# Input sums one channel pair earlier, the u tile formed on GpSimd, token weights stored permuted

## The chip, the cores and the metric

The kernel runs on one core of one Trainium2 chip. The metric is device time in microseconds for one launch; lower is better. The program works on eight samples one after the other, so most of the time is spent in a steady pattern that repeats once per sample.

## The reference

The input `x` has 8 samples of 3008 tokens and 256 channels, all float32. First a global filter along the tokens, then an MLP mixer: a token product with a residual, then a channel product with a residual.

```python
X = np.fft.rfft(x, axis=1)                     # x: (8, 3008, 256)
Y = X * (filt_r + 1j * filt_i)[None]
x = np.fft.irfft(Y, n=3008, axis=1)
h = np.maximum(x.transpose(0, 2, 1) @ w_tok1, 0.0) @ w_tok2    # w_tok1 (3008, 256), w_tok2 (256, 3008)
u = x + h.transpose(0, 2, 1)
out = u + np.maximum(u @ w_ch1, 0.0) @ w_ch2                   # w_ch1 (256, 1536), w_ch2 (1536, 256)
```

## The kernel before

**The mixer.** `mix` walks over 288 *items* (b, m, jp): sample b (0 to 7), block m of 512 tokens (0 to 5, the last of 448), and pair jp of 128-wide tiles of the hidden channels (0 to 5). The products are 2 by 2 block products done with seven multiplications instead of eight, so sums and differences of operands and of results have to be made by VectorE (the helper `v`, L997). In one item TensorE does, in this order: `up_first` (L1019, four products into two banks called pg), part 0 of `down` for the item before, `up_last` (L1035, three products into the same two banks), part 1 of `down` and part 2 of `down` (L1053). VectorE in the same item does `up_middle` (tiles hh and s, read from pg), the sums t of the item before (`h_sums`: one of 512 elements, two of 256, all from the on-chip tile hh), and two results hh out of pg. ScalarE copies one result and takes the two ReLUs.

Between these stand places (0, 1, 1.5, 1.7, 2) at which `mix` yields, and at which other work is put in:

- The next block's operand u, made at jp = 2 and 3 by `u_quarter` in parts 0 to 3 (at jp = 4 for the first block of the next sample). Its even and odd parts come out of PSUM by VectorE; `u_turn` (L943 to L953) then turns them in place into their sum and difference with two VectorE instructions of 512 elements; `v_steps` makes the sums v out of u. `u_turn` and `v_steps` are put into a list, and `one_step` takes two entries of it per item, after `up_last`.
- The finished block's results (`finish`): four steps of sums and two transposes, then 16 stores whose DMAs are issued by GpSimd (L1065) at jp = 2 and 3.
- The filter of the sample after next, `dft`, from sample 1 on beside the mixer. Its first stage has six channel pairs of input. For each, `next_sum` has VectorE make sum and difference of two loaded tiles (L563, two instructions of 512 elements; the results, tiles p1 and p2, alternate), then loads another pair on SyncE's queue; `sets` multiplies them (L538 on sd, eight products of quarter arrays) into two banks, either the pg pair or the pair acc and b (`turn`); ScalarE copies the banks out, SyncE stores them to z. Later stages (steps "b", "m", "i") have two sets per channel quad.

Which filter step comes at which place is written by hand in the last lines of the kernel: a table gives (jp, place) for each step, and `tail` is the last block of a sample. The letters are those that `dft` yields: "s" a sum, "e" a single pair's sets, "d" two pairs' sets, "c" the copies out of acc and b, "w" loads of filters and tables.

Before the change the first stage runs so: sum 0 at (3, 1) and sets 0 at (4, 1.5) of the tail; sums 1 and 2 at (0, 1) and (1, 1), sets 1 and 2 together at (1, 1.5) of the next sample's first block; sums 3 and 4 at (2, 1) and (3, 1), sets 3 at (3, 1.5) on the pg banks; sum 5 at (4, 1) and sets 4 and 5 at (4, 1.5).

**The token product** (`token_product`) runs once per sample at jp = 2 of the last block, from weights in `w1_d`, a scratch tensor in DRAM. `w1_sums` writes it during sample 0: the raw rows and the sums that GpSimd makes of them, in eight DMAs issued by GpSimd. `w1_load` reads it back, twelve slices per sample, each in two DMAs on SyncE's queue, one for each half of the partitions, with the rows permuted on the way.

Of the kernel before, what the change touches and what calls it, by code (L numbers as in the profile page):

```python
# [10 lines left out]
FP32 = mybir.dt.float32  # L11
# [3 lines left out]
ALU = mybir.AluOpType  # L15


B = 8
# [5 lines left out]
P = 128  # L24
# [19 lines left out]
JP = JT // 2  # L44
DH = D // P
CW = 32
CB = P // CW
MT = 6
# [5 lines left out]
W1S = 7  # L54
# [78 lines left out]
def kernel(  # L133
# [11 lines left out]
    nc = tc.nc  # L145
# [19 lines left out]
    w1_d = nc.dram_tensor("w1_tmp", (AP, P, 7, P), FP32, kind="Internal").ap()  # L165
# [14 lines left out]
    up = pool("up", 2)  # L180
    hp = pool("hp", 2)
    tp = pool("tp", 2)
    vp = pool("vp", 2)
# [10 lines left out]
    turn = ["acc", "b"]  # L194
# [17 lines left out]
    w1_ring = w1_all.rearrange("p (r s t) -> p r s t", s=7, t=P)  # L212
# [327 lines left out]
    def half_of(half, n=HALF):  # L540
        return slice(half * HALF, half * HALF + n)
# [34 lines left out]
    def dft(bs):  # L576
        first = bs[0] == 0
# [21 lines left out]
        def zero_rows(c):  # L599
            nc.gpsimd.memset(filts[c], 0.0)  # L600

        def w_load(c):
            table_load(c)
            (filt_load if first else filt_quad)(c)
# [15 lines left out]
        def next_sum():  # L620
            i = len(sums)
            sums.append(x_sums(*todo[i], i))
            more(1)

        def sets(i, n, banks_of):
            return [a_pair(*u, sd, tags) for u, sd, tags in zip(todo[i:i + n], sums[i:], banks_of)]

        if tiled:
            next_sum()
            for i in (0, 3):  # L630
                yield "e"
                sets(i, 1, (("pg", "pg"),))[0]()
                for _ in range(2 if i == 0 else 1):
                    yield "s"
                    next_sum()
                yield "d"
                leave, leave_pg = sets(i + 1, 2, (turn, ("pg", "pg")))
                leave_pg()
                yield "c"
                leave()  # L640
                for _ in range(2 * (i == 0)):
                    yield "s"
                    next_sum()
                    if len(sums) == 4:
                        zero_rows(0)
                        w_load(0)
            yield "w"
        for i, u in enumerate(() if tiled else todo):
            if first and i in (0, 2):
# [152 lines left out]
    def w1_sums():  # L802

        w = w1.rearrange("p (j r) (t n) -> p j r t n", r=2, n=P)
        to = w1_d.rearrange("j p s n -> p j s n")

        def raw_out():
            nc.gpsimd.dma_start(to[:, :, 0], w[:, :, 0, 0])
            nc.gpsimd.dma_start(to[:, :, 1:3], w[:, :, 1])

        def pool(out, in0, in1, op):
            return lambda: nc.gpsimd.tensor_tensor(out=out, in0=in0, in1=in1, op=op)

        todo = [raw_out]
        for j in range(0, AP, 3):
            c11, c21, c12, c22 = (w[:, j:j + 3, r, t] for r in range(2) for t in range(2))
            todo += [pool(c22, c21, c22, ALU.add), pool(c21, c11, c21, ALU.subtract),
                     pool(c11, c22, c11, ALU.subtract), pool(c12, c12, c11, ALU.subtract)]

        def sums_out(j):  # L820
            return lambda: nc.gpsimd.dma_start(to[:, j:j + 2, 3:7], w[:, j:j + 2].rearrange("p j r t n -> p j (r t) n"))

        return todo, [sums_out(j) for j in range(0, AP, 2)]

    def w1_load(j):
        rows = w1_d[j].rearrange("(k h g) s n -> h k g (s n)", h=2, g=2)
        for h in range(2):
            nc.sync.dma_start(w1_ring[half_of(h), j % W1S], rows[h])

    token_ts, todo_h1 = {}, []  # L830

# [47 lines left out]
    def width(m):  # L879
        return 512 if m < MT - 1 else 448  # L880
# [8 lines left out]
    def u_unit(b, m, h1, ut, dh):  # L889

        w = width(m)
        ps = bank(free_bank())
        for t in range(TC):
            nc.tensor.matmul(ps[:, 0:w], h1[:, t, ts(dh, P)], w2[:, t, ds(m * 512, w)],
                             start=(t == 0), stop=False)
        u_filter(b, m, dh, ps, False)
        nc.scalar.copy(out=ut[:, dh, 0:w], in_=ps[:, 0:w])
# [42 lines left out]
            for e in range(2):  # L940
                v(us[:, :, e], pss[e], us[:, :, e])

    def u_turn(ut):  # L943
        us = ut.rearrange("p d (e n) -> p d e n", e=2)
        plus, minus = us[:, :, 0], us[:, :, 1]

        def first():
            v(plus, plus, minus)

        def second():  # L950
            nc.vector.scalar_tensor_tensor(out=minus, in0=minus, scalar=-2.0, in1=plus, op0=ALU.mult, op1=ALU.add)

        return [first, second]  # L953

    def w2m_load(m):
        nc.sync.dma_start(w2m[m % 2], w2_d[m])
# [39 lines left out]
    def v(out, in0, in1, op=ALU.add):  # L996
        nc.vector.tensor_tensor(out=out, in0=in0, in1=in1, op=op)  # L997
# [7 lines left out]
    def u_sums(ut, vt, w):  # L1005
        hw = w // 2
        return sums(vt[:, :, 0:hw], ut[:, :, hw:w], ut[:, 0, 0:w].rearrange("p (s n) -> p s n", s=2),
                    ut[:, 0, 0:hw], ut[:, 1, 0:hw])
# [138 lines left out]

    def u_part(b, m, i):
        if i == 0:
            uts[b, m] = up.tile([P, DH, 512], FP32, tag="u", name="u")  # L1150
        (u_quarter if b else u_unit)(b, m, h1s[b], uts[b, m], i)

    def v_steps(b, m):
        vts[b, m] = vp.tile([P, 4, 256], FP32, tag="v", name="v")
        t13, t2, t4_ = u_sums(uts[b, m], vts[b, m], width(m))

        def t24():
            t2()
            t4_()

        return [t13, t24]

    todo_v = []

    def one_step():
        if todo_v:
            todo_v.pop(0)()

    def mix(next_ready):
# [14 lines left out]
        def u_parts(b, m, jp, place):  # L1184
            parts = own[b > 0] if m + 1 < MT else new if b + 1 < B else {}
            now = parts.get((jp, place), ())
            b, m = (b, m + 1) if m + 1 < MT else (b + 1, 0)
            for part in now:
                u_part(b, m, part)
            if now and now[-1] == max(p for ps in parts.values() for p in ps):  # L1190
                if m:
                    wait.append(m)
                if b:
                    todo_v.extend(u_turn(uts[b, m]))
                todo_v.extend(v_steps(b, m))
                if b and (b, m) < (B - 1, MT - 2):
                    w2m_load((m + 2) % MT)
# [5 lines left out]
        for i in range(len(items) + 1):  # L1203
# [70 lines left out]
            if now:  # L1274
                if b + 1 < B and i % n == n - 4:
                    h1s[b + 1] = yield from token_product(b + 1)
                u_parts(b, m, jp, 2)
                if m + 1 == MT and jp == JP - 2 and b + 1 < B:
                    one_step()
                    one_step()  # L1280
                if jp == JP - 1:
                    while todo_v and m + 1 == MT:
                        one_step()
                if i >= 8 and to_dram:
                    to_dram.pop(0)()
                if i in (28, 29):
                    w2m_load(i - 28)
                if i == 28:
                    nc.sync.dma_start(wai[:, 0:HALF], was_i_d)
# [5 lines left out]
    with tc.manual_schedule():  # L1295
# [71 lines left out]
        for b, i, place in mix(next_ready):  # L1367
            at = (b, i, place)
            if at == (0, 0, 0) or group + 1 < len(GROUPS) and at == (GROUPS[group][-1], n - 4, 2):
                if not done:  # L1370
                    raise AssertionError("the filter's steps don't fit beside the mixer's")
                group += 1
                done = group + 1 == len(GROUPS)
                todo = iter(()) if done else dft(GROUPS[group + 1]) if group else second
                coming = next(todo, "end") if group else "a"
                if group:
                    continue
            if done or place == 1.7 and coming != "m":
                continue
            jp = i % JP  # L1380
            if coming in "aw":
                due = place == 1 or (place != 1.5 if group == 0 else coming == "w")
            else:
                tail = i >= n - JP
                due = i >= JP * (group == 0) and (jp, place) in {
                    "s": ((3, 1),) if tail else ((0, 1), (1, 1), (2, 1), (3, 1), (4, 1)),
                    "e": ((4, 1.5),) if tail else ((3, 1.5),), "d": ((1, 1.5), (4, 1.5)), "c": ((2, 0), (5, 0)),
                    "b": ((1, 1.5), (4, 1.5)), "m": ((2, 1.7) if tail else (3, 1), (5, 1)), "i": ((0, 1.5), (4, 1.5))}[coming]
            if coming == "a" and group == 0 and i < JP - 1:
                due = place in (0, 2)  # L1390
            for _ in range(due):
                if not done:
                    coming = next(todo, "end")
                    done = coming == "end"
# [30 lines left out]
```

## Time and profile before

| | |
|---|---|
| Runs | 2453.93, 2454.04, 2458.0 us; median 2454.04 us |
| Profiled execution | 2460.43 us, of which the span of the trace is 2458.7 us |
| Granted TensorE clock over the span | 0.993 |
| Busy share of the span | TensorE 97%, VectorE 82%, GpSimd 29%, ScalarE 28% |
| VectorE, `u_turn`'s two instructions | 42 x 682 ns and 42 x 692 ns |
| GpSimd, issue of an output store | 738 x 623 ns |
| GpSimd, sum of 512 elements per partition (L966) | 18 x 1350 ns |

The page gives the busy time of each engine, the time cut into slices, DMA queues and the costliest groups of instructions. A group's line ends with the idle time of its engine just before its instructions and what ended that idle time. The view of waits lists the same by waiter and releaser: us in total, how often, the longest. A timeline lists instructions in order of time: start, duration and, in square brackets, the idle time before it with its releaser; a float32 matmul leaves two records, so "x8" are four products. TensorE's durations overlap, because matmuls are pipelined: two records of 128x256 that follow one another start 0.216 us apart at full clock, and 0.427 us apart at half clock.

### The profile page before, as it was taken

To read this page: it belongs to the slowest core of one execution; us is meant where nothing else is said; L and a number is where in the kernel's file an instruction comes from. 1 tells how busy PE (TensorE), PEld (TensorE's weight loads), DVE (VectorE), ACT (ScalarE), POOL (GpSimd) and SP (SyncE) were. 2 spreads that over 40 slices of the span, in tenths; PEclk is the share of its full clock that TensorE was granted. 3 is DMA by queue.
4 is the path that set the end of the run, shared out by engine and by line. 5 is a ranking of instruction groups with operands and counts; after the bars stand their busy time and mean duration, and the time that the engine had idled before them with its cause. 6 is when DMAs were issued, how large, how long until landed. Compare 5 with 4: busy or idle time off the path is not lost.

```text
span 2458.7 us, 41273 instructions
## 1 busy us (share of the span) xinstructions
PE 2379.9 (97%) x15148; PEld 1983.3 (81%) x15148; DVE 2011.5 (82%) x3753; ACT 689.4 (28%) x1339; POOL 705.6 (29%) x1117
## 2 busy tenths in 40 slices
PE   7989999999999999999999999999999999999998
PEld 4667678778897888978888788877888788898887
DVE  7798887778877888778887788877887788878786
ACT  5732222222222222222221222222222222212222
POOL 7486644121221122212212221222122112212222
PEclk8999999999999999999999999999999999999999
DMA  9964347343463334533345433644346333441101
GB/s 213 247 179 138 119 140 211 111 126 89 108 188 121 99 102 128 172 117 96 108 125 152 128 106 98 177 116 124 92 108 187 116 105 101 129 130 30 48 14 21
DMA packets 191088, 302.35 MB, mean 123 GB/s; under 512 B 44100, under 2 KB 127402, under 8 KB 185510
## 3 DMA queue, kind: packets, MB, share of 16 engines
q1 hardware_dynamic: 144238, 237.62, 33.2%
q0 software_dynamic: 40032, 55.28, 9.5%
q10 hardware_dynamic: 6616, 6.82, 0.9%
q8 instruction: 120, 1.97, 0.4%
q14 instruction: 82, 0.67, 0.1%
HBM read 215.40 MB, written 83.62 MB: 122 GB/s over the span
## 4 chain that ended last, share of the span: by engine, by line
PE 71%; DVE 10%; DMA 9%; POOL 4%; issue 3%; ACT 2%; SPq 1%; DVEq 0%; ACTq 0%; POOLq 0%
PE ps_po L1053 28%; PE ps_pg L1019 16%; PE ps_pg L1035 12%; PE ps_acc L925 3%; DVE t L997 3%; PE ps_pg L538 3%; PE ps_b L538 2%; POOL out_dram L1065 2%; DMA z_tmp<-t 2%; DVE hh L997 2%; PE ps_b L925 2%; DMA out_dram<-r 1%; DVE u L997 1%; PE ps_b L851 1%; PE ps_acc L905 1%
## 5 line engine op out<-in xcount | busy, mean ns | idle before, releaser
L1065 POOL DMA_DIRECT2D out_dram<-r x738 | 453.3, 623 | 1536.6 <-issue 981.2
L1040 ACT ACTIVATE hh<-hh 128x512 f32<-128x512 f32 (+1 forms) x576 | 347.7, 621 | 1017.8 <-DVE hh L997 1014.0
L997 DVE TENSOR_TENSOR hh<-ps_pg,s 128x512 f32<-128x512 f32 (+3 forms) x864 | 481.6, 585 | 153.6 <-ACT s L1022 143.8
L1053 PE MATMUL ps_po<-t,wc 128*128 128x256 f32 (+1 forms) x2296 | 566.8, 381 | 3.4 <-DVE t L997 3.3
L1053 PEld LDWEIGHTS ps_po<-t,wc 128*128 128x128 f32 x2296 | 426.6, 191 | 97.2 <-issue 32.2
L1019 PE MATMUL ps_pg<-v,wc 128*128 128x256 f32 (+1 forms) x1728 | 418.8, 379 | 7.0 <-DVE v L997 5.3
L1053 PE MATMUL ps_po<-hh,wc 128*128 128x256 f32 (+1 forms) x1722 | 411.9, 375 | 0.6 <-POOL wc L396 0.6
L1019 PEld LDWEIGHTS ps_pg<-v,wc 128*128 128x128 f32 x1728 | 326.1, 191 | 57.1 <-DVE v L997 19.1
L1053 PEld LDWEIGHTS ps_po<-hh,wc 128*128 128x128 f32 x1722 | 327.4, 190 | 38.3 <-POOL wc L396 1.4
L1035 PE MATMUL ps_pg<-u,wc 128*128 128x256 f32 (+1 forms) x1152 | 292.6, 377 | 7.4 <-DVE hh L997 7.3
L997 DVE TENSOR_TENSOR t<-t,hh 128x256 f32<-128x256 f32 (+1 forms) x576 | 254.9, 442 | 19.8
L1035 PEld LDWEIGHTS ps_pg<-u,wc 128*128 128x128 f32 x1152 | 216.1, 190 | 41.8 <-DVE hh L997 15.3
L997 DVE TENSOR_TENSOR s<-ps_pg,hh 128x512 f32<-128x512 f32 (+1 forms) x288 | 196.0, 681 | 30.7 <-DVE hh L997 0.9
L1022 ACT COPY s<-ps_pg 128x256 f32<-128x256 f32 (+1 forms) x288 | 105.9, 368 | 337.9 <-PE ps_pg L1019 336.1
L997 DVE TENSOR_TENSOR t<-hh 128x512 f32<-128x512 f32 (+1 forms) x288 | 196.4, 682 | 0.6 <-ACT hh L1040 0.6
L1019 PE MATMUL ps_pg<-u,wc 128*128 128x256 f32 (+1 forms) x576 | 171.2, 379 | 6.6 <-DVE hh L997 3.9
L1035 PE MATMUL ps_pg<-v,wc 128*128 128x256 f32 (+1 forms) x576 | 168.8, 375 | 0.0
L1019 PEld LDWEIGHTS ps_pg<-u,wc 128*128 128x128 f32 x576 | 108.2, 191 | 26.3 <-DVE hh L997 8.4
L997 DVE TENSOR_TENSOR u<-ps_acc,u 128x256 f32<-128x256 f32 x84 | 46.8, 557 | 98.6 <-PE ps_acc L925 76.1
L1035 PEld LDWEIGHTS ps_pg<-v,wc 128*128 128x128 f32 x576 | 108.4, 190 | 13.4
L925 PE MATMUL ps_acc<-w 128*128 128x256 f32 x336 | 97.5, 392 | 0.0
L717 DVE TENSOR_TENSOR p<-ps_b,filt 128x1024 f32<-128x1024 f32 x56 | 68.4, 1222 | 14.5 <-PE ps_pg L538 11.4
(169 smaller groups left out, 2801.6 us busy)
## 6 DMA issues: line engine op xcount, KB each, us to landing
w<-w_tmp SPq DMA_DIRECT2D x42, 1024.0 KB
w<-w_tmp SPq DMA_DIRECT2D x168, 224.0 KB
out_dram<-r POOLq DMA_DIRECT2D x738, 32.0 KB, 4.3
g_tmp<-t SPq DMA_DIRECT2D x112, 192.0 KB
t<-g_tmp SPq DMA_DIRECT2D x42, 512.0 KB
t<-z_tmp SPq DMA_DIRECT2D x196, 96.0 KB
z_tmp<-t SPq DMA_DIRECT2D x72, 256.0 KB
wb<-wbi_t SPq DMA_DIRECT2D x56, 256.0 KB
```

What stands on the lines that cost most here:

```text
L538: nc.tensor.matmul(outs(i, j), stat(i, j), mov(i, j), start=True, stop=True)
L717: nc.vector.tensor_tensor(out=prods[c, h], in0=pss[h].unsqueeze(1).to_broadcast([P, 2, 2, D]), in1=filts[c % FB], op=ALU.mult)
L851: nc.tensor.matmul(ps[:, at], w[:, n], mov, start=(j == 0 and i in (0, 2)), stop=(j == AP - 1 and i >= 5))
L905: nc.tensor.matmul(pss[e][half_of(i), dh, ts(q, HALF)], t4[b, c][half_of(e), r, ds(dh * P + i * HALF, HALF)], wai[half_of(e), 0:HALF], sta ...
L925: nc.tensor.matmul(to, h1[:, n, :], w2_at(m, at), start=(i < 2 and j == 0), stop=(j >= 1))
L997: nc.vector.tensor_tensor(out=out, in0=in0, in1=in1, op=op)
L1019: nc.tensor.matmul(ps[:, 0:hw], chan[0][:, jp, n, :], mov, start=True, stop=True)
L1022: nc.scalar.copy(out=s[:, 0], in_=g[0][:, 0, 0:hw])
L1035: nc.tensor.matmul(ps[:, 0:hw], chan[0][:, jp, n, :], mov, start=True, stop=True)
L1040: nc.scalar.activation(out=hs, in_=hs, func=AF.Relu)
L1053: nc.tensor.matmul(po[i][:, j, 0:hw], chan[1][:, jp, n, :], mov, start=(jp == 0 and first == 1), stop=(jp == JP - 1 and last == 1))
L1065: q.dma_start(bass.AP(tensor=ob.tensor, offset=ob.offset + to, ap=ap + [[1, cw]]), of)
```

## The change

1. In `dft`, sums 0 and 1 stand before the first sets, and from then on every sum stands one pair further ahead. The table's "s" becomes (3, 1), (4, 1), (5, 1) in the tail and (0, 1), (2, 1), (3, 1) otherwise, its "e" becomes (4, 1.5) and (5, 1.5), without regard to the tail. Sets 1 then run alone in the tail, on acc and b; sets 2 and 3 together at (1, 1.5), sets 4 and 5 together at (4, 1.5). Clearing and loading the first filter tile (`zero_rows(0)`, `w_load(0)`) moves from after sum 3 to after sets 3.
2. From sample 1 on, `u_quarter` writes the even and odd parts into the tile that will hold v, and GpSimd makes u from them with two instructions (sum and difference, 512 elements each), issued right after the parts. `v_steps` then overwrites the even and odd parts. The two VectorE steps, and the two `one_step` calls that made room for them at the sample's end, go.
3. `w1_sums` writes the rows of `w1_d` in the order in which they are read, four DMAs for each one before (32 in all), on SyncE's queue; `w1_load` is one DMA.

```diff
         if tiled:
             next_sum()
-            for i in (0, 3):
+            yield "s"
+            next_sum()
+            for i in range(2):
                 yield "e"
-                sets(i, 1, (("pg", "pg"),))[0]()
-                for _ in range(2 if i == 0 else 1):
+                sets(i, 1, (turn if i else ("pg", "pg"),))[0]()
+                yield "s"
+                next_sum()
+            for i in (2, 4):
+                yield "d"
+                leave, leave_pg = sets(i, 2, (turn, ("pg", "pg")))
+                leave_pg()
+                if i == 2:
+                    zero_rows(0)
+                    w_load(0)
+                yield "c"
+                leave()
+                for _ in range(2 * (i == 2)):
                     yield "s"
                     next_sum()
-                yield "d"
...
-                    if len(sums) == 4:
-                        zero_rows(0)
-                        w_load(0)
             yield "w"
...
         def raw_out():
-            nc.gpsimd.dma_start(to[:, :, 0], w[:, :, 0, 0])
-            nc.gpsimd.dma_start(to[:, :, 1:3], w[:, :, 1])
+            for i in range(4):
+                nc.sync.dma_start(to[i][:, :, 0], w[i::4, :, 0, 0])
+                nc.sync.dma_start(to[i][:, :, 1:3], w[i::4, :, 1])
...
     def w1_load(j):
-        rows = w1_d[j].rearrange("(k h g) s n -> h k g (s n)", h=2, g=2)
-        for h in range(2):
-            nc.sync.dma_start(w1_ring[half_of(h), j % W1S], rows[h])
+        nc.sync.dma_start(w1_ring[:, j % W1S], w1_d[j])
...
-    def u_turn(ut):
-        us = ut.rearrange("p d (e n) -> p d e n", e=2)
-        plus, minus = us[:, :, 0], us[:, :, 1]
-
-        def first():
-            v(plus, plus, minus)
-
-        def second():
-            nc.vector.scalar_tensor_tensor(out=minus, in0=minus, scalar=-2.0, in1=plus, op0=ALU.mult, op1=ALU.add)
-
-        return [first, second]
+    def u_turn(b, m):
+        plus, minus = (vts[b, m].rearrange("p d (e n) -> p d e n", e=2)[:, :, e] for e in range(2))
+        uts[b, m] = up.tile([P, DH, 512], FP32, tag="u", name="u")
+        us = uts[b, m].rearrange("p d (h n) -> p d h n", h=2)
+        return [lambda: nc.gpsimd.tensor_tensor(out=us[:, :, 0], in0=plus, in1=minus, op=ALU.add),
+                lambda: nc.gpsimd.tensor_tensor(out=us[:, :, 1], in0=plus, in1=minus, op=ALU.subtract)]
...
                 if b:
-                    todo_v.extend(u_turn(uts[b, m]))
+                    for f in u_turn(b, m):
+                        f()
                 todo_v.extend(v_steps(b, m))
...
-                if m + 1 == MT and jp == JP - 2 and b + 1 < B:
-                    one_step()
-                    one_step()
...
-                    "s": ((3, 1),) if tail else ((0, 1), (1, 1), (2, 1), (3, 1), (4, 1)),
-                    "e": ((4, 1.5),) if tail else ((3, 1.5),), "d": ((1, 1.5), (4, 1.5)), "c": ((2, 0), (5, 0)),
+                    "s": ((3, 1), (4, 1), (5, 1)) if tail else ((0, 1), (2, 1), (3, 1)),
+                    "e": ((4, 1.5), (5, 1.5)), "d": ((1, 1.5), (4, 1.5)), "c": ((2, 0), (5, 0)),
```

More of the change, by code (lines that the diff above doesn't have):

```diff
@@ L629, in dft @@
             next_sum()
-            for i in (0, 3):
+            yield "s"
+            next_sum()
+            for i in range(2):
                 yield "e"
-                sets(i, 1, (("pg", "pg"),))[0]()
-                for _ in range(2 if i == 0 else 1):
+                sets(i, 1, (turn if i else ("pg", "pg"),))[0]()
[11 more added lines that the diff above has]
+                for _ in range(2 * (i == 2)):
                     yield "s"
                     next_sum()
-                yield "d"
[L637 to L643, printed above, removed]
-                    if len(sums) == 4:
-                        zero_rows(0)
-                        w_load(0)
             yield "w"
@@ L804, in w1_sums @@
         w = w1.rearrange("p (j r) (t n) -> p j r t n", r=2, n=P)
-        to = w1_d.rearrange("j p s n -> p j s n")
+        to = [w1_d.rearrange("j (h k g) s n -> h g k j s n", h=2, g=2)[i // 2, i % 2] for i in range(4)]
         def raw_out():
-            nc.gpsimd.dma_start(to[:, :, 0], w[:, :, 0, 0])
-            nc.gpsimd.dma_start(to[:, :, 1:3], w[:, :, 1])
+            for i in range(4):
+                nc.sync.dma_start(to[i][:, :, 0], w[i::4, :, 0, 0])
+                nc.sync.dma_start(to[i][:, :, 1:3], w[i::4, :, 1])
         def pool(out, in0, in1, op):
@@ L820, in sums_out, with f @@
         def sums_out(j):
-            return lambda: nc.gpsimd.dma_start(to[:, j:j + 2, 3:7], w[:, j:j + 2].rearrange("p j r t n -> p j (r t) n"))
+            def f():
+                for i in range(4):
+                    nc.sync.dma_start(to[i][:, j:j + 2, 3:7], w[i::4, j:j + 2].rearrange("p j r t n -> p j (r t) n"))
+            return f
         return todo, [sums_out(j) for j in range(0, AP, 2)]
     def w1_load(j):
-        rows = w1_d[j].rearrange("(k h g) s n -> h k g (s n)", h=2, g=2)
-        for h in range(2):
-            nc.sync.dma_start(w1_ring[half_of(h), j % W1S], rows[h])
+        nc.sync.dma_start(w1_ring[:, j % W1S], w1_d[j])
     token_ts, todo_h1 = {}, []
@@ L1149, in u_part @@
         if i == 0:
-            uts[b, m] = up.tile([P, DH, 512], FP32, tag="u", name="u")
-        (u_quarter if b else u_unit)(b, m, h1s[b], uts[b, m], i)
-    def v_steps(b, m):
-        vts[b, m] = vp.tile([P, 4, 256], FP32, tag="v", name="v")
-        t13, t2, t4_ = u_sums(uts[b, m], vts[b, m], width(m))
+            where, tag = (vp, "v") if b else (up, "u")
+            to = uts if b == 0 else vts
+            to[b, m] = where.tile([P, DH, 512], FP32, tag=tag, name=tag)
+        if b:
+            u_quarter(b, m, h1s[b], vts[b, m], i)
+        else:
+            u_unit(b, m, h1s[b], uts[b, m], i)
+    def v_steps(b, m):
+        if b == 0:
+            vts[b, m] = vp.tile([P, 4, 256], FP32, tag="v", name="v")
+        vt = vts[b, m] if b == 0 else vts[b, m].rearrange("p d (s n) -> p (d s) n", s=2)
+        vts[b, m] = vt
+        t13, t2, t4_ = u_sums(uts[b, m], vt, width(m))
         def t24():
```

## Prediction, made before the changed kernel was run

> **What bounds the kernel now.** I read the page first, then the waits of TensorE, then timelines of single stretches, and last the start times of every item's first up product (L1019 on u).
>
> ```profile
> PE 2379.9 (97%) x15148; PEld 1983.3 (81%) x15148; DVE 2011.5 (82%) x3753; ACT 689.4 (28%) x1339; POOL 705.6 (29%) x1117
> ```
>
> TensorE is the bound, so only its waits can be won. The view of waits says whom it waits for:
>
> ```profile
> PE ps_pg L538 <- DVE sd L563: 17.4, 12, 1.7
> ...
> PE ps_pg L1035 <- DVE hh L997: 7.3, 10, 1.6
> PE ps_pg L1019 <- DVE v L997: 5.3, 7, 0.8
> ...
> PE ps_pg L1019 <- ACT t L554: 2.8, 6, 1.1
> PE ps_b L851 <- DMA w<-w_tmp: 2.4, 4, 0.9
> ```
>
> The largest is the input sets waiting for their sums, twice in each of six samples. The timelines of TensorE and VectorE show such a place, jp = 1 of a first block:
>
> ```profile
> 1053.48 0.65 PE L538 MATMUL ps_b<-sd,was 64*64 64x512 f32 x2
> ...
> 1056.30 1.59 PE L538 MATMUL ps_pg<-sd,was 64*64 64x512 f32 x8 [1.73 <-DVE sd L563]
> 1057.82 1.96 PE L1053 MATMUL ps_po<-t,wc 128*128 128x256 f32 x4
> 1059.58 1.06 PE L1019 MATMUL ps_pg<-u,wc 128*128 128x256 f32 x2
> ```
> ```profile
> 1053.14 1.28 DVE L997 TENSOR_TENSOR hh<-ps_pg,s 128x512 f32<-128x512 f32 x2
> 1054.34 1.22 DVE L997 TENSOR_TENSOR u<-u,r 128x224 f32<-128x224 f32 x3
> 1055.47 1.28 DVE L563 TENSOR_TENSOR sd<-filt 128x512 f32<-128x512 f32 x2
> ```
>
> The banks pg are free when the hh results are out, at 1054.42; the sets start 1.88 us later, behind sum 2. After the wait TensorE also runs at half clock (two products in 1.96 us instead of 1.03), for 3.41 us. That happens in three of six samples.
>
> The item lengths, from one first up product to the next, are very regular. A plain item takes 6.04 us (sample 7, where no filter runs); one with filter sets "b" 8.13. Against that, jp = 0 of a block takes 6.24: TensorE waits 0.20 for v, hidden in pipelined records. jp = 0 of a sample's first block takes 6.70. jp = 1 of the first block takes 11.02 (11.82, 12.51 and 12.67 with half clock), and jp = 4 there 10.35 to 11.30, mean 10.65.
>
> **The change, part by part.** The sum is made against the profiled execution, 2460.43 us (span 2458.7, 1.7 around it). The median of the runs is 6.4 lower. The half-clock stretches make 5.0 of that if the median run lacks them: 1.64, 0.79 and 1.48 over 11.03, and 0.90 and 0.16 more in the items behind the last two.
>
> *Sums ahead.* Sum 2 moves to (5, 1) of the tail, sum 3 to (0, 1), sum 5 to (3, 1). Only the pg banks then hold the second set back. At jp = 1 the gap from the end of the acc and b sets (last start 1053.98, plus 0.47) to 1056.30 is 1.85 us; 0.6 more lies in small waits of that item, of which I take half: 2.15 x 6 samples = 12.9 us. At jp = 4 the same gap is 1.29; the mean of 10.65 holds 0.25 more of waits on ScalarE's copies, and small ones: 1.7 x 6 = 10.2. Without any wait both items would be 6.04 + 0.96 (acc and b) + 1.40 (pg) + 0.15 = 8.55 us, so the ends are 14.8 and 12.6, and 0 if pg comes late anyway. Sets 1 leave jp = 3 (10.77 against 9.49, so 1.28 us) for the tail, where a set on acc and b is about 1.05, with its two z stores (SyncE, 0.7 us each): 0.
>
> *Half clock.* It follows the longest of these gaps, and goes with them: 5.0 in the profiled execution, 0 against the median. [...]
>
> *What the moved sums push.* Two sums (1.28 us each) now stand in the tail at jp = 4 and 5, one at jp = 0. At jp = 4 VectorE idles 3.59 us right there, which hides the first; without that cover it would hold up the parts of u behind it by 1.28. The other two have `finish` behind them, whose results nothing waits for, and then `up_middle`, which TensorE does wait for. Adding up VectorE's instructions from 1041 us on, it reaches jp = 1 some 0.6 us late for `up_last`: 0.6 x 6 = 3.6 us, between 0 and 7. Each sum issues its six loads earlier on SyncE's queue (0.60, 0.51, 0.26 us, twice); behind them are w2 and z transfers, and TensorE's waits above name none of those: 0. The first filter tile is cleared (0.97 us) ahead of the 16 stores on GpSimd, no longer behind them, and SyncE's loads of it, which waited up to 12.2 us for that, come earlier: 0.
>
> *u on GpSimd.* VectorE loses 42 x (682 + 692) ns = 57.7 us, worth something only where TensorE waits for it. v moves from the end of jp = 5 to the end of jp = 4, an item before it is needed: 0.20 x 35 blocks = 7.0 us. At a sample's start v stays at jp = 5, with less in front of it: half of 0.66 x 7, 2.3 us.
>
> The price is what GpSimd's sums do to VectorE's. Sample 0 has the row, on GpSimd and on VectorE:
>
> ```profile
> 383.74 4.14 POOL L966 TENSOR_TENSOR w<-w 128x512 f32<-128x512 f32 x3
> ```
> ```profile
> 383.55 2.03 DVE L997 TENSOR_TENSOR t<-hh 128x512 f32<-128x512 f32 x1
> 385.61 2.56 DVE L997 TENSOR_TENSOR t<-t,hh 128x256 f32<-128x256 f32 x2
> 388.09 1.27 DVE L997 TENSOR_TENSOR hh<-ps_pg,s 128x512 f32<-128x512 f32 x2
> ```
>
> The t sums, whose operands are both on chip, take 4.6 us instead of 1.57; hh, with an operand in PSUM, is untouched. Each GpSimd sum on top of t costs VectorE about 1.0 us. Where would the new ones lie? In block 2 of sample 2, at the end of jp = 3, the last part of the next u is out at 878.26, and GpSimd is still issuing stores:
>
> ```profile
> 868.78 4.37 POOL L1065 DMA_DIRECT2D out_dram<-r  x8 [34.42 <-ACT u L931]
> 873.81 5.46 POOL L1065 DMA_DIRECT2D out_dram<-r  x8 [0.66 <-DMA out_dram<-r]
> ```
>
> It is free at 879.27; over the blocks, 0.1 to 2.4 us after u's last part, mostly 0.5 to 1.2. Two sums of 1.35 us end at about 882. The t sums of jp = 4 run from 880.29 to 881.9, so the second GpSimd sum lies on them, the first hardly: VectorE is late by 1.0 us, between 0 (done before t) and 2.7 (both fully in front of t). hh is out at 883.09, and the sets that follow on pg start at 883.82, so 0.73 are covered. 30 items have such sets (four blocks with "b" and one with input sets, six samples): 30 x (1.0 - 0.73) = 8.1 us. In sample 7's five there is 1.35 us of cover: 0. VectorE asks for u at 883.1 + 1.0, GpSimd is done at 882: no wait there.
>
> [...] In the row VectorE's instructions end 0.3 to 0.6 us after GpSimd's, so they overlap in part. [...]
>
> *Token weights.* 84 loads on SyncE instead of 168; TensorE waits 2.4 us for them in all: 0, at most 2.4 won. The 32 writes (0.4 us each, 12.8 us of queue) replace eight issues on GpSimd (6.5 us). The first eight stand before loads of z for which SyncE waits until 198.7 us anyway, the others in stretches where it idles (304.8 to 316.5): 0, up to 3 if that cover fails.
>
> Sum: 12.9 + 10.2 + 7.0 + 2.3 - 3.6 - 8.1 = 20.7 us off the median, 2454.0 - 20.7 = 2433.3; with the half clock 25.7 off the profiled execution, 2434.7. I say 2434.
>
> **Rivals.** *GpSimd's sums lie on t.* If the stores keep GpSimd longer, or its sums run slower than 1.35 us, VectorE is late by 2.7 in each jp = 4: 30 x 1.97 + 5 x 1.35 = 66 us against the other terms' 28.8, so 37 slower, 2491. It decides from a delay of 0.73 + 28.8 / 30 = 1.69 us on. For it speaks the row above, where three sums cost 3.0; against it that hh and s read PSUM, and that the first sum falls on those. 9%.
>
> *The wait only changes its name.* [...] For it speaks VectorE at 82%; against it the 1.88 us between hh's end and the set's start. 10%.
>
> *Sums don't move ahead.* The order of instructions excludes it: sum 3 stands a whole item before sets 2 and 3 on VectorE. 1%.
>
> **How the numbers follow.** The forecast has 80%. Its low end, with all waits gone and no lock, is 2454.0 - (14.8 + 12.6 + 7.0 + 4.6) = 2415; I take 2418. The upper end reaches to the rivals' first part, 2456, and leaves out the case of 2491. A measurement can tell about 0.2%, 4.9 us, from no change: faster 0.80, same 0.10, slower 0.10.
>
> **What would show it.** L538's wait for sd gone from TensorE's waits, and jp = 1 and 4 of first blocks at 8.6 to 9.2 us; jp = 0 at 6.04; no half clock inside the mixer; GpSimd's two sums ending before VectorE's v; the t sums of jp = 4 longer by about 1 us, and "b" items there at 8.4. Wrong would be "b" items at jp = 4 above 9 us, or L538 waiting for hh instead of sd for over 10 us.

## The result

The changed kernel takes 2414.49 us, the median of 4 runs (2412.96 to 2415.46), against 2455.15 (2453.93 to 2458.0) for the kernel before: a ratio of 0.9832, 95% interval 0.9815 to 0.9849. The medians are 40.7 us apart where 20.7 were forecast; the profiled executions (2460.43 and 2413.99 us) are 46.4 apart, forecast 25.7. The direction was right, the range did not hold the time: 2414 lies below its low end of 2418.

**The profile after.** The page's line of engines: VectorE has lost 84 instructions but only 12 us of busy time, because others of its instructions became longer, its t sums above all (the first of the three in each item: 196.4 us before, 233.0 now, over all items).

```profile
PE 2361.0 (98%) x15148; PEld 1979.2 (82%) x15148; DVE 1999.9 (83%) x3669; ACT 689.9 (29%) x1339; POOL 805.5 (33%) x1193
```

TensorE's waits. "L538 <- DVE sd" (17.4 us before) is gone, and little stands in its place: the sets now wait for hh, 2.6 us in all. The wait for v fell from 5.3 to 0.8.

```profile
PE ps_po L1053 <- DVE t L997: 5.7, 13, 0.7
...
PE ps_pg L1035 <- DVE hh L997: 5.0, 6, 1.4
...
PE ps_pg L538 <- DVE hh L997: 2.6, 6, 1.0
...
PE ps_pg L1019 <- DVE v L997: 0.8, 1, 0.8
```

The timeline of TensorE at jp = 1 of the same first block as before (sample 3). The set on pg now starts 0.43 us after the one on b and acc instead of behind a gap, and the next part of `down` follows 1.09 us later, at full clock:

```profile
1036.09 0.59 PE L538 MATMUL ps_b<-sd,was 64*64 64x512 f32 x2
...
1036.52 1.16 PE L538 MATMUL ps_pg<-sd,was 64*64 64x512 f32 x8
1037.61 1.13 PE L1053 MATMUL ps_po<-t,wc 128*128 128x256 f32 x4
1038.58 0.59 PE L1019 MATMUL ps_pg<-u,wc 128*128 128x256 f32 x2
```

Item lengths (first up product to next first up product), after minus before, summed over samples 1 to 6 of the two profiled executions, beside the forecast's terms sorted into the same places:

| Items | Forecast, us | Measured, us |
|---|---|---|
| jp = 1, 2 of first blocks (half clock included) | -17.9, pushed sums +3.6 | -17.9 |
| jp = 4 of first blocks | -10.2, GpSimd's sums +1.6 | -15.2 |
| start of a sample: jp = 5 of the tail, jp = 0 and 3 of the first block | -2.3 | -7.1 |
| jp = 0 of later blocks (v earlier) | -7.0 | -5.7, and -0.95 in sample 7 |
| jp = 1 of later blocks | 0 | -2.5 |
| jp = 4 of blocks 1 to 4 (GpSimd's sums) | +6.5 | +16.5 |
| jp = 2, 3 of the tail | 0 | -6.5 |
| sample 0, and what stands before it | 0 | -6.3 |
| sum | -25.7 | -45.7 of the 46.4 |

jp = 1 is now 8.82 to 9.12 us, jp = 4 of the first block 8.12, jp = 0 of a sample 5.67. No stretch at half clock is left in samples 1 to 6.

### The profile page after: what moved, and what is told of

It is laid out like the page before. It is cut to its first block, busy times and chain, and to the rows that moved or that the text cites. A ratio compares the mean times of both kernels' runs of the same rounds, so it can differ in the third digit from the quotient of the medians.

```text
span 2412.2 us, 41264 instructions
## 1 busy us (share of the span) xinstructions
PE 2361.0 (98%) x15148; PEld 1979.2 (82%) x15148; DVE 1999.9 (83%) x3669; ACT 689.9 (29%) x1339; POOL 805.5 (33%) x1193
## 3 DMA queue, kind: packets, MB, share of 16 engines
q1 hardware_dynamic: 148014, 243.12, 32.6%
q10 hardware_dynamic: 6616, 6.82, 0.9%
## 4 chain that ended last, share of the span: by engine, by line
PE 83%; DVE 9%; DMA 3%; issue 2%; POOL 1%; ACT 1%; SPq 0%; DVEq 0%; ACTq 0%; POOLq 0%
PE ps_po L1053 32%; PE ps_pg L1019 18%; PE ps_pg L1035 13%; PE ps_acc L930 3%; PE ps_b L856 3%; DVE t L997 3%; PE ps_pg L538 3%; PE ps_b L538 3%; PE ps_acc L856 2%; PE ps_b L930 2%; DVE hh L997 2%; PE ps_acc L910 1%; DVE s L997 1%; DVE sd L563 1%; DMA x<-in_x_dram 1%
## 5 line engine op out<-in xcount | busy, mean ns | idle before, releaser
L1019 PE MATMUL ps_pg<-v,wc 128*128 128x256 f32 (+1 forms) x1728 | 412.6, 375 | 2.2 <-POOL wc L395 1.5
L997 DVE TENSOR_TENSOR t<-t,hh 128x256 f32<-128x256 f32 (+1 forms) x576 | 259.9, 451 | 19.8
L997 DVE TENSOR_TENSOR t<-hh 128x512 f32<-128x512 f32 (+1 forms) x288 | 233.0, 809 | 0.6 <-ACT hh L1040 0.6
L1035 PE MATMUL ps_pg<-v,wc 128*128 128x256 f32 (+1 forms) x576 | 168.8, 375 | 0.0
L997 DVE TENSOR_TENSOR v<-ps_acc,v 128x256 f32<-128x256 f32 x84 | 46.9, 558 | 85.2 <-PE ps_acc L930 61.4
L997 DVE TENSOR_TENSOR u<-ps_po,u 128x512 f32<-128x512 f32 (+1 forms) x142 | 79.1, 585 | 0.0
```

Source lines behind the costliest of these rows:

```text
L1019: nc.tensor.matmul(ps[:, 0:hw], chan[0][:, jp, n, :], mov, start=True, stop=True)
L1035: nc.tensor.matmul(ps[:, 0:hw], chan[0][:, jp, n, :], mov, start=True, stop=True)
```

## The experiments

**The three parts, alone and in pairs.** Six kernels divide the change: part 1 is the input sums, part 2 u on GpSimd, part 3 the token weights. Each is the kernel before with those hunks of the change. Each ratio here and further down is to runs of the kernel before that were taken together with that experiment's (medians 2456.05, 2456.95 and 2457.01 us), so the ratios, not the medians, are to be compared across tables.

Part 1 alone:

```diff
-            for i in (0, 3):
+            yield "s"
+            next_sum()
+            for i in range(2):
...
-                    "s": ((3, 1),) if tail else ((0, 1), (1, 1), (2, 1), (3, 1), (4, 1)),
+                    "s": ((3, 1), (4, 1), (5, 1)) if tail else ((0, 1), (2, 1), (3, 1)),
```

> Only the first part of the change: sums one pair ahead, u still turned by VectorE, w1 as before. Theory A (the sets waited for their sums, and each part removes its own waits): jp = 1 of first blocks falls from 11.0 to 12.7 us to about 8.9, jp = 4 from 10.65 to 8.2 to 8.6, no half clock in the mixer, jp = 0 stays at 6.24; 25 to 32 us off, 2423 to 2430. Rival B (VectorE as a whole was late, and its relief by GpSimd is what did it): the sets then wait for hh on the pg banks, jp = 4 stays above 9.5, no more than 12 us off, 2443 or more.

Part 2 alone:

```diff
-                    todo_v.extend(u_turn(uts[b, m]))
+                    for f in u_turn(b, m):
+                        f()
...
-                    one_step()
-                    one_step()
```

> Only the second part: GpSimd forms u, sums and w1 as before. [...] Rival B (VectorE's 58 us less work is what shortens the waits elsewhere): 10 us or more faster, 2445 or less.

Part 3 alone:

```diff
-        for h in range(2):
-            nc.sync.dma_start(w1_ring[half_of(h), j % W1S], rows[h])
+        nc.sync.dma_start(w1_ring[:, j % W1S], w1_d[j])
```

> Only the third part: w1 written permuted on SyncE, read with one DMA. Theory A (the 6.5 us that the changed kernel lost at jp = 2 and 3 of the tails, and part of sample 0's 4, come from the loads): those items at 24.15 and 5.30, 6 to 10 us off, 2445 to 2449. Rival B (these tails are shorter because VectorE and GpSimd are ahead): no change, 2455 within 2.

Parts 1 and 2 (the changed kernel with the third diff undone):

```diff
-        nc.sync.dma_start(w1_ring[:, j % W1S], w1_d[j])
+        for h in range(2):
+            nc.sync.dma_start(w1_ring[half_of(h), j % W1S], rows[h])
```

> First and second part without the third. Theory A (the third part is worth the tail's 6.5 us and some of sample 0): 2421 to 2424. Rival B (it is worth nothing): 2414 to 2416.

Parts 1 and 3 (the changed kernel with the second undone):

```diff
-                    for f in u_turn(b, m):
-                        f()
+                    todo_v.extend(u_turn(uts[b, m]))
```

> First and third part without the second: VectorE turns u as before. [...] Rival B (without the relief VectorE is late for the pg banks in first blocks and at the samples' start): 2420 or more.

Parts 2 and 3 (the changed kernel with the first undone):

```diff
-                    "s": ((3, 1), (4, 1), (5, 1)) if tail else ((0, 1), (2, 1), (3, 1)),
+                    "s": ((3, 1),) if tail else ((0, 1), (1, 1), (2, 1), (3, 1), (4, 1)),
```

> Second and third part without the first. If the parts add, this is the changed kernel plus what the first part is worth alone: with 25 to 32 us for that, 2440 to 2447. If the sums ahead work only together with GpSimd's u, 2425 to 2435.

| Parts | Median, us | Ratio to before, 95% interval |
|---|---|---|
| 1 | 2417.89 | 0.9837 (0.9819 to 0.9856) |
| 2 | 2471.23 | 1.0053 (1.0036 to 1.0070) |
| 3 | 2445.20 | 0.9947 (0.9931 to 0.9963) |
| 1, 2 | 2425.14 | 0.9869 (0.9851 to 0.9888) |
| 1, 3 | 2408.53 | 0.9803 (0.9787 to 0.9820) |
| 2, 3 | 2461.04 | 1.0016 (1.0007 to 1.0025) |
| 1, 2, 3 | 2414.49 | 0.9832 (0.9815 to 0.9849) |

What follows:

- Part 1 makes nearly the whole gain. Its items alone change by -18.3 (jp = 1, 2), -15.2 (jp = 4) and -7.8 us (start of a sample): the first three rows of the table, without any relief by GpSimd.
- Part 2 costs 0.3 to 0.7% in all four comparisons (against nothing, part 1, part 3, and both); the two of 0.3% are little more than their intervals. Its items show both sides: -5.7 at jp = 0, -2.5 at jp = 1, and +16.3 at jp = 4 of blocks 1 to 4. Without part 1 it is worst: alone it makes jp = 4 of the first block 5.7 us longer in six samples. Most of that is half clock: four of these six items have a stretch with a granted clock of 0.5 for 3.41 us and take 11.65 to 12.34 us, the other two 10.70 and 11.16. In the kernel before no such stretch falls there.
- Part 3 brings 0.3 to 0.5% wherever it is added: 4.0 to 6.4 us at jp = 2 and 3 of the tails of samples 1 to 6, and 4.2 to 6.7 us in sample 0, of which 1.1 to 2.7 in its tail.
- The expectation held for part 3 (2445 to 2449), and parts 1 and 3, at 2408.53, contradict the rival's 2420 or more. Part 1 was faster than its 2423 to 2430, parts 1 and 2 were a little slower than their 2421 to 2424, and part 2 alone, at 2471.23, is far from its rival's 2445 or less. Parts 2 and 3 missed by most: 14 us above the 2440 to 2447, because part 1 is worth more beside them (1.8%) than the 25 to 32 us put in for it.

How part 1 shortened the start of a sample can be read in two timelines of TensorE. Before, the first item of sample 3 stood 0.76 us before its v products:

```profile
1041.06 0.60 PE L1019 MATMUL ps_pg<-u,wc 128*128 128x256 f32 x2
1042.41 1.56 PE L1019 MATMUL ps_pg<-v,wc 128*128 128x256 f32 x6 [0.76 <-DVE v L997]
```

After, sets 1 stand in the item ahead, and the v products follow at once:

```profile
1022.39 0.59 PE L538 MATMUL ps_b<-sd,was 64*64 64x512 f32 x2
...
1022.93 1.02 PE L1053 MATMUL ps_po<-t,wc 128*128 128x224 f32 x4
1023.79 0.59 PE L1019 MATMUL ps_pg<-u,wc 128*128 128x256 f32 x2
1024.22 1.46 PE L1019 MATMUL ps_pg<-v,wc 128*128 128x256 f32 x6
```

jp = 0 is 5.67 us with part 1 alone too, where VectorE still turns u. So the moved set did not add its length: it gives TensorE work while VectorE makes v, where TensorE stood idle. In six samples jp = 3 lost 7.7 us and jp = 0 6.2, and jp = 5 of the tail gained 6.75.

**Who holds up VectorE.** In the changed kernel GpSimd issues the output stores of the finished block first and u's sums after them. This kernel issues the stores of blocks 0 to 3 behind the sums:

```diff
+            if b and m < MT - 2:
+                held.append(send)
+            else:
+                send()
...
                     for f in u_turn(b, m):
                         f()
+                    while held:
+                        held.pop(0)()
```

> The changed kernel, but for blocks 0 to 3 the 16 stores are issued after GpSimd's two sums instead of before. Theory A (the stores hold GpSimd until 0.5 to 2.4 us after u's parts, and so its sums meet VectorE's t sums): GpSimd's sums start 0.15 us after the parts in every block, VectorE's first t sum ends at about +3.2 instead of up to +4.2, all b items at jp = 4 take 8.13, and 14 to 17 us go: 2398 to 2401. [...] Rival C (late stores hold up the tile r and the next block): slower, over 2420.

It takes 2400.07 us, ratio 0.9769 (0.9753 to 0.9785). The one place that changes in samples 1 to 6 is jp = 4 of blocks 1 to 4: -16.3 us, 23 of the 24 items are back at 8.13. The same place in both kernels, the end of jp = 3 in block 3 of sample 2, shows it. In the changed kernel GpSimd is free late:

```profile
901.70 4.77 POOL L1065 DMA_DIRECT2D out_dram<-r  x7 [0.90 <-issue]
906.48 1.28 POOL L952 TENSOR_TENSOR u<-v 128x512 f32<-128x512 f32 x1
907.71 1.73 POOL L953 TENSOR_TENSOR u<-v 128x512 f32<-128x512 f32 x1
```
```profile
906.84 1.48 DVE L997 TENSOR_TENSOR t<-hh 128x512 f32<-128x512 f32 x1
908.36 1.83 DVE L997 TENSOR_TENSOR t<-t,hh 128x256 f32<-128x256 f32 x2
910.11 1.28 DVE L997 TENSOR_TENSOR hh<-ps_pg,s 128x512 f32<-128x512 f32 x2
```

The set on pg waits for that hh, and the item is 9.24 us long:

```profile
910.84 1.68 PE L538 MATMUL ps_pg<-p,wb 64*64 64x256 f32 x16 [0.29 <-DVE hh L997]
```

With the stores held, GpSimd starts 0.15 us after u's last part, and its second sum ends 0.6 us after t begins:

```profile
901.78 1.27 POOL L952 TENSOR_TENSOR u<-v 128x512 f32<-128x512 f32 x1 [32.47 <-DVE v L997]
903.01 1.26 POOL L953 TENSOR_TENSOR u<-v 128x512 f32<-128x512 f32 x1
904.22 7.79 POOL L1065 DMA_DIRECT2D out_dram<-r  x13
```
```profile
903.66 1.16 DVE L997 TENSOR_TENSOR t<-hh 128x512 f32<-128x512 f32 x1
904.86 0.88 DVE L997 TENSOR_TENSOR t<-t,hh 128x256 f32<-128x256 f32 x2
905.66 1.28 DVE L997 TENSOR_TENSOR hh<-ps_pg,s 128x512 f32<-128x512 f32 x2
```

The three t sums take 1.57 us undisturbed; here 2.04, which the set on pg covers, and 3.31 in the changed kernel.

The next kernel leaves the stores where the change has them and replaces each of GpSimd's sums by two fills of the same tile. It leaves out u's values, so its products have other operands.

```diff
-        return [lambda: nc.gpsimd.tensor_tensor(out=us[:, :, 0], in0=plus, in1=minus, op=ALU.add),
...
+        return [lambda: nc.gpsimd.memset(us[:, :, 0], 0.5), lambda: nc.gpsimd.memset(us[:, :, 0], 0.5),
...
```

> The changed kernel, but GpSimd's two sums are four fills of the same halves of u with a constant (u's values are left out): GpSimd writes but reads nothing. Theory A (VectorE's t sums are held back by GpSimd reading on chip): the first t sum keeps 0.68 us, b items at jp = 4 take 8.13, 2397 to 2400. Rival B (any GpSimd instruction that long holds VectorE's sums): t sums at 1.2 to 2.2 us as in the changed kernel, 2410 or more.

It takes 2397.92 us, ratio 0.9759 (0.9740 to 0.9777). GpSimd is busy beside t as before, for 4 x 0.53 us, but the 512-element t sums (groups with shapes kept apart) fall from 824 ns to 698, the 695 of the kernel before, and jp = 4 of blocks 1 to 4 loses 16.5 us. The changed kernel's group, and two of this one:

```profile
L997 DVE TENSOR_TENSOR t<-hh 128x512 f32<-128x512 f32 x240 | 197.8, 824 | 0.0
```
```profile
L952 POOL MEMSET u<- 128x512 f32 x84 | 44.7, 532 | 2.4
...
L997 DVE TENSOR_TENSOR t<-hh 128x512 f32<-128x512 f32 x240 | 167.6, 698 | 0.0
```

So it is not GpSimd being busy that makes t longer, but something that the sums do and the fills do not. Reading on chip is the difference that stands out; a GpSimd instruction that reads a single operand was not tried. With the stores behind the sums, part 2 pays: 0.9769 against 0.9803 for parts 1 and 3 without it.

**What part 3 does.** In the kernel before, ScalarE's first copy of the token product (tile c, in a buffer that output stores have read) waits in six of seven tails for those stores to finish; in the changed kernel it waits for the product alone, some 18.6 us each time. So of the 121.5 us below, about 10 are due to the stores (121.5 - 6 x 18.6). The views of ScalarE's waits of the two:

```profile
ACT c L859 <- DMA out_dram<-r: 121.5, 6, 21.4
```
```profile
ACT c L864 <- PE ps_b L856: 129.9, 7, 18.6
```

Three kernels ask which edit does it. The first reads each slice in two DMAs of 64 partitions again, but in stored order:

```diff
-        nc.sync.dma_start(w1_ring[:, j % W1S], w1_d[j])
+        for h in range(2):
+            nc.sync.dma_start(w1_ring[half_of(h), j % W1S], w1_d[j, half_of(h)])
```

> The changed kernel, but each slice of the token weights is read in two DMAs again, one for each half of the partitions (64 each), the rows staying in stored order. Theory A: what made ScalarE's c copies of the tail wait for output stores is the 64-partition form of these loads (in the kernel before they took 13.61 us of DMA time a step against 5.01 us). Then tail jp = 2 and 3 lose most of their 6.5 us over samples 1 to 6 again and ScalarE waits for stores: 2418 to 2422. Rival B: it was the row order with its small pieces; then the items stay as in the changed kernel: 2412 to 2416.

The second also uses two DMAs, each of all 128 partitions:

```diff
-        nc.sync.dma_start(w1_ring[:, j % W1S], w1_d[j])
+        for lo, hi in ((0, 4), (4, 7)):
+            nc.sync.dma_start(w1_ring[:, j % W1S, lo:hi], w1_d[j, :, lo:hi])
```

> The changed kernel, but each slice of the token weights is read in two DMAs that both cover all 128 partitions (columns 0 to 3 and 4 to 6). Theory A (partitions per DMA decide): no loss, 2412 to 2416, tail jp = 3 at 5.30 us. Rival B (two DMAs instead of one, whatever their shape, take the queue from the stores' neighbours): as many issues as in the run with half the partitions, so the same loss as there, 2418 to 2422.

The third moves the writes of sample 0 to GpSimd:

```diff
-                nc.sync.dma_start(to[i][:, :, 0], w[i::4, :, 0, 0])
-                nc.sync.dma_start(to[i][:, :, 1:3], w[i::4, :, 1])
+                nc.gpsimd.dma_start(to[i][:, :, 0], w[i::4, :, 0, 0])
+                nc.gpsimd.dma_start(to[i][:, :, 1:3], w[i::4, :, 1])
```

> The changed kernel, but the 32 writes of the token weights in sample 0 are issued by GpSimd instead of SyncE. Theory A: the gain of the token weights' part comes from reading alone; samples 1 to 7 as in the changed kernel, sample 0 within 1 us: 2413 to 2416. Rival B: sample 0's 4.0 us came from GpSimd being rid of eight issues; 32 issues there cost these 4 us and more: 2418 or above.

| Kernel | Median, us | Ratio to before, 95% interval |
|---|---|---|
| two DMAs of 64 partitions | 2425.18 | 0.9871 (0.9857 to 0.9884) |
| two DMAs of 128 partitions | 2416.24 | 0.9832 (0.9819 to 0.9846) |
| writes by GpSimd | 2417.29 | 0.9837 (0.9823 to 0.9850) |

By the times the 64-partition form gives back all that part 3 won (0.9869 without it); the median lies a little above the 2418 to 2422 expected. (The 13.61 and 5.01 us in that expectation are stretches of SyncE's queue with 12 issues and with 4, not the same step in two forms.) By the items it gives back 7.2 us: 4.7 in the tails of samples 1 to 6 and 2.5 in the tail of sample 0. The item jp = 3 of the tail is 5.98 to 6.82 us instead of 5.30, and ScalarE waits for stores again, in three tails by name:

```profile
ACT c L865 <- PE ps_pg L1020: 60.7, 3, 21.4
ACT c L865 <- DMA out_dram<-r: 59.0, 3, 20.2
```

The last store before the copy lands 0.8 to 1.5 us after the first up product of jp = 3 in the tails of samples 0 to 5; in the changed kernel it lands 0.2 to 1.4 us before it. The chain from there, in the tail of sample 3: VectorE waits for the copy, and TensorE for the hh that stands behind on VectorE (timelines of both).

```profile
1292.68 0.42 DVE L998 TENSOR_TENSOR c<-ps_b,c 128x256 f32<-128x256 f32 x1 [4.04 <-ACT c L865]
```
```profile
1294.31 1.02 PE L1036 MATMUL ps_pg<-u,wc 128*128 128x224 f32 x4 [0.68 <-DVE hh L998]
```

In the changed kernel VectorE's wait at this place is 2.43 us, and TensorE has none. With 64 partitions the row order adds nothing to this: the tails lose 4.9 us in six samples with permuted rows (parts 1 and 2) and 4.7 in stored order. The number of DMAs and the place of the writes don't matter either: the second and third kernel lie a little above 2416, the upper end of what was expected, with ratios that cannot be told from the changed kernel's; jp = 2 and 3 of the tail differ from it by 0.0 and 0.2 us in six samples. The 3 to 4 us that part 3 wins in sample 0 outside its tail stay in all three kernels (at most 0.7 us of them is lost), so what makes them is none of these three edits; it was not traced. The packets of SyncE's queue, the same 243.12 MB, take 34.6% of the DMA engines' span with 64 partitions, 33.2% with two DMAs of 128 and 32.6% with one. Why the form with 64 partitions takes longer is in no view.

**A version in between.** The kernel with held stores, but with VectorE making the u of each sample's first block:

```diff
+        q = nc.gpsimd if m else nc.vector
...
+                if m + 1 == MT and jp == JP - 2 and b + 1 < B:
+                    one_step()
+                    one_step()
```

> The run with held stores (2400.07 us), but the u of each sample's first block is made by VectorE as in the kernel before, with the two extra list steps at the sample's end. Theory A: GpSimd's sums at jp = 5 of the tail hold up VectorE there; tail jp = 5 goes from 6.75 us to about 6.1, 4 us in six samples: 2395 to 2398. Rival B: VectorE's own two instructions (1.37 us a sample) stand in front of what jp = 0 of the next sample waits for; jp = 0 goes from 5.67 back to 6.3 or more: 2400 to 2405.

It takes 2396.98 us, ratio 0.9760 (0.9746 to 0.9773), which cannot be told from 0.9769. The time lies in theory A's range, but theory A named the right place and the wrong size: jp = 5 of the tail goes from 6.75 to 6.51 us, 1.4 in six samples and not 4; the rest of that item's growth is the set. Rival B's loss at jp = 0 does not appear, 5.67 as before. Both versions with held stores beat the changed kernel, by 14.5 us of the profiled span at the first (2412.2 and 2397.7 us).

## Why the prediction was right, and where it was wrong

The time lies below the range because gains were left out or sized too small: the token weights, put at 0, were worth some 10 us, the waits at jp = 4 of the first block 15.2 instead of 10.2, the start of a sample 7.1 instead of 2.3. GpSimd's sums cost VectorE's twice the 8.1 and hid part of this. Even the sum behind the low end, 2415 with all waits gone and these 8.1 left out, lies above the 2414.49 that were measured with their cost. No run shows a "lock", as that sum calls it; the traces show t sums that end some 0.56 us after GpSimd's.

**Right: the waits for sums vanish and the half clock with them.** jp = 1 and 2 lost 17.9 us, 12.9 + 5.0 to the tenth, and the tenth is luck: the set on pg starts 1.91 us earlier behind the sets on acc and b and takes 1.09 us instead of 1.52, 14.0 in six samples, of which the moved sums take some 1 back (below). In samples 1 to 6 none of the ten kernels with part 1 has a stretch at half clock (granted clock 0.5); the four without it, which keep the gaps, have three (the kernel before), six (part 2), one (part 3) and five (parts 2 and 3), of 3.41 us each. Here the 5.0 went with gaps of 1.9 us. Which gap sets off the half clock stays open: in the kernel before the gap at jp = 1 is the same in all six samples, and the half clock follows in three. v earlier was worth 5.7 and 0.95 us against 7.0; the 2.5 us at jp = 1 of later blocks, which part 2 alone wins too, were not in the prediction.

**Wrong, jp = 4 of the first block, 10.2 against 15.2.** The low end of "without any wait both items would be 8.55" was taken as a floor. The set on pg took 1.52 us behind its wait; when nothing holds it, it takes 0.97 us at jp = 4 and 1.09 at jp = 1 (1036.52 to 1037.61). The prediction had 1.40 for it in that floor and nothing in the sum. These 0.55 us are most of the 0.83 missed per item; the rest lies in the waits behind the set, 0.63 us instead of 0.4, and in the gap. The item is 8.12, the length that the "b" items showed all along. The prediction had that 8.13 in hand.

**Wrong, what the moved sums push, +3.6 against some 1.** With part 1 alone `up_last` of jp = 1 starts 3.33 us after the item's first product, against 3.20 before and 3.02 where nothing holds it: 0.13 x 6 = 0.8 us, and sample 3 of the changed kernel has 0.3 more. jp = 0 shows no loss (5.67). VectorE's instructions were added up from the order before, without the work that TensorE got in the tail; that this is the whole of the error is not shown.

**Wrong, the start of a sample, -2.3 against -7.1.** Sets 1 were said to cost in the tail what they save at jp = 3. They do, but they stand where TensorE would have waited for v: the step missed that a moved set can fill a wait. The 2.3 us forecast for VectorE's relief there did not come: with part 2 alone jp = 0 stays at 6.70 and jp = 5 of the tail is 0.7 us longer in six samples.

**Wrong, GpSimd's sums on VectorE's, +8.1 against +16.5.** The prediction counted 30 items with VectorE late by 1.0 and 0.73 covered. Measured from the start of v after u's last part (4.74 us undisturbed), VectorE is late by 1.31 on average in the 24 items of blocks 1 to 4 (0.49 to 2.43), and about 0.64 is covered: a lateness of 0.49 leaves the item at 8.13, 0.88 makes it 8.36, 0.94 8.42, 2.43 9.91. 24 x 0.67 is 16.1. In the first block's six, GpSimd starts at once (lateness 0.49) and nothing is lost. The lateness goes with the start of GpSimd's first sum after u's last part: 0.49 at 0.15 us, 0.88 at 0.52, 2.43 at 2.36. The mis-sized term is the time at which GpSimd becomes free, which the prediction had read as 0.1 to 2.4 us and then replaced by one middle value. The sums overlap less than "in part" suggests: in the item above the first t sum starts at 906.84, GpSimd's sum ends at 907.76, t at 908.32. So t ends 0.56 us after GpSimd's sum, most of the 0.68 that it takes alone.

**Wrong, the token weights, 0 against some 10.** "TensorE waits 2.4 us for them: 0, at most 2.4" looked for the loads' own wait. Their effect was on other transfers: stores finished late, ScalarE's copy waited for a buffer, VectorE for the copy, TensorE for VectorE at jp = 2 and 3 of the tail, as the experiment with 64 partitions shows. The view of ScalarE's waits of the kernel before has this line, 121.5 us by name, some 10 more than the product alone takes; the prediction followed TensorE's own waits only. Sample 0 gained 4.0 us, 2.4 of it at jp = 2 of its own tail; what made the rest was not traced. The other 2.3 of the 6.3 stand before the mixer's first product, which comes at 138.4 us in the changed kernel and at 138.5 to 143.0 in the six that differ from it only behind that point, so they are scatter.

**The rivals.** GpSimd's sums on t was the real danger: it took 16.5 us of part 1's gain, without turning the sign. The table's rows differ from the forecast by 20 us in sum; the largest single miss, the 10.0 of GpSimd's sums, went the other way, and six smaller ones together outweighed it. The wait that only changes its name did not come: L538 waits 2.6 us for hh. What the upper end of 2456 took from that rival is shown by no run; the runs with the sums ahead have 1.0 to 2.6 us of that wait. Of the signs that the prediction named for being wrong one did come: ten of the 24 "b" items at jp = 4 of blocks 1 to 4 stand above 9 us, with a mean of 8.82 where 8.4 was said.

## What to carry to other kernels

Ask of a moved piece of work not only what it costs where it lands, but whether the bottleneck waits there anyway. Before giving GpSimd an elementwise sum, look at what is queued in front of it: here the same two instructions cost 16.5 us behind eight store issues and 0.2 ahead of them. And look at the waits of idle engines for buffers whose stores are late: here loads of 64 partitions cost 4.7 us in six tails through them, where TensorE's own waits for the loads of the kernel before were 2.4 us in all.

## What the runs showed of the hardware

- Beside a GpSimd sum of two on-chip operands, t, a VectorE sum of on-chip tiles, took 1.48 us instead of 0.68 and ended 0.56 us after GpSimd's sum. s, a VectorE sum with an operand in PSUM, took 0.69 us beside the same GpSimd sum, and hh 0.68 beside one of sample 0 (343.79 in the changed kernel), both as without. Beside GpSimd fills of 0.53 us each t took 698 ns on average, against 695 in the kernel before and 824 in the changed one.
- In the same item GpSimd's second sum, begun while t ran, took 1.73 us instead of the 1.26 with the stores held, and the next t sum of 256 elements 1.37 instead of 0.42.
- Reading the same bytes in two DMAs of 64 partitions rather than 128 cost this kernel 0.4% (0.9871 against 0.9832); the median time from a store's issue to its landing was 4.4 us against 4.1.
- TensorE ran at half clock for 3.41 us behind gaps of 1.9 us, in three of six samples of the kernel before; without the gaps it did not in samples 1 to 6 of ten kernels.
